# Fused attention and maxout FFN on one core: q and k transposed once on TensorE for groups 3 to 6, x of batch 1 on TensorE, output weights loaded later

## The chip, the cores and the metric

One core of one Trainium2 chip. The metric is the device time of one execution in microseconds (us), the median of several runs. Each run also reports a span (first to last instruction, about 1.9 us less than the device time) and the mean granted TensorE clock. A run over 1.5% above the fastest of its kernel is called slow and is left out of every ratio here.

Engines: PE is TensorE's matmuls, PEld its weight loads, DVE is VectorE, ACT is ScalarE, POOL is GpSimd, SP is SyncE, which here issues DMAs. A trailing q (POOLq, SPq) marks an engine's sequencer, for example when it issues a DMA. TensorE's results go to PSUM in this kernel, and another engine copies them out (an evacuation or eviction; in after the VectorE copies `hT<-p_i` are 48, of 0.62 us each). KT and QT are the transposed k and q, AV is the product of attention and v, and the up work or up pieces are the products with w1, w2 and w3.

## The reference, cut to what matters

```python
# q, k, v: (8 batches, 12 heads, 448 rows, 64)
scores = scale * q @ k.T
m = max(scores)
e = exp(scores - m)
attn = e / (sum(e) + exp(-m) + 1e-9)
x = (attn @ v) as (8 * 448, 768)
h = max(x @ w1, x @ w2, x @ w3)      # 768 x 768 each
out = h @ w_out                      # (3584, 768), float32
```

## The kernel before

The heads are taken in 24 groups of four heads, three groups to a batch; group `i` belongs to batch `i // 3`. Groups 0 to 2 are done in two halves, E and O, so that the FFN of batch 0 can start early; from group 3 on, each group takes three "visits" of score units. Between the steps of attention, `fill` puts pieces of FFN work (up projection, then output projection) into TensorE's program. The order in the program is the order in which an engine runs its instructions in the traces here, and a waiting instruction holds up those behind it.

The kernel's scores take q and k with the head dimension on partitions, in two arrangements of q. Groups 0 to 5 were transposed on TensorE, both arrangements of q (15 transposes) and k (7):

```python
PE_QK = 6          # groups below this are transposed on TensorE

def transpose_pe(i, pr, pool, k_eng, q_engs):     # pr 0 and 1: two halves
    ...
    kj = (0, 1, 2) if pr == 0 else (3, 4, 5, 6)
    qt = (-1, 1, 3, 5, 0, 2, 4, 6) if pr == 0 else (8, 10, 12, 7, 9, 11, 13)
    ...                                            # transposes to PSUM, then copies to KT, QT
```

From group 6 on, a DMA transpose makes one arrangement and GpSimd copies the shifted one (`shift_q`). x goes through DMA transposes from batch 1 on. The loads are issued in order by GpSimd:

```python
for n, (part, g) in enumerate(parts):     # E0 E1 E2 O0 O1 O2
    ...
    if n == 1:
        load_weight(2)
    if n == 2:
        load_v(3)
        load_qk(4)
        load_weight(3)                     # the output weights
    if n == 4:
        load_v(4)
        load_qk(5)
        transpose_pe(3, 0, ps_s, DV, (DV,))
...
for i in range(3, NI):
    ...
    for vi, units in enumerate(visits):
        scores(i, ej, units)
        ...
        if vi > 0 and i + 1 < PE_QK:       # the next group's q and k, in visits 1 and 2
            fill(per / 2)
            transpose_pe(i + 1, vi - 1, ps_s, DV, (DV,))
            fill(per / 2)
        else:
            fill(per)
```

The softmax here doesn't subtract the row's maximum and nothing guards it: scores larger than these inputs give would overflow.

Of the kernel before, what the change touches and what calls it, by code (L numbers as in the profile page):

```python
# [21 lines left out]
def kernel(  # L22
# [29 lines left out]
    scale = 1.0 / math.sqrt(D)  # L52


    PE_QK = 6
    NEB = 2
    NV = 3

# [9 lines left out]
    )  # L68

    cpool = ctx.enter_context(tc.tile_pool(name="const", bufs=1))  # L70
    ld_pool = ctx.enter_context(tc.tile_pool(name="ld", bufs=4))
    att_pool = ctx.enter_context(tc.tile_pool(name="att", bufs=3))
    small = ctx.enter_context(tc.tile_pool(name="small", bufs=3))
    xn_pool = ctx.enter_context(tc.tile_pool(name="xn", bufs=3))
# [12 lines left out]

    groups = [(b, g) for b in range(B) for g in range(NG)]
    raw = {}

    def load_qk(i, names="kq", prs=(0, NP)):
        b, g = groups[i]
        tiles = raw.setdefault(i, {})
        for nm in names:
            if nm not in tiles:
                t = ld_pool.tile([P, NP * T + 2, D], MMDT, tag="ld_" + nm, name="ld_" + nm)
                if nm == "q" and i < PE_QK:
                    nc.vector.memset(t[:, 0 : NP * T + 2 : NP * T + 1, :], 0.0)
                tiles[nm] = t
            src = {"q": q, "k": k}[nm][b].rearrange("h s d -> (h s) d")  # L100
            src = src.rearrange("(g r x t) d -> g x r (t d)", g=NG, r=NP, x=P)[g]
            p0, p1 = prs
            nc.gpsimd.dma_start(  # L103
                out=tiles[nm][:, 1 : NP * T + 1].rearrange("x (r t) d -> x r (t d)", r=NP)[:, p0:p1],
                in_=src[:, p0:p1],
            )

    def load_v(i):
        b, g = groups[i]
        t = ld_pool.tile([P, GH, 5, D], MMDT, tag="ld_v", name="ld_v")  # L110
        raw.setdefault(i, {})["v"] = t
        src = v[b].rearrange("(g h) (p t) d -> g p h (t d)", g=NG, t=T)[g]
        nc.gpsimd.dma_start(  # L113
            out=t[0:HP, :, 1:5].rearrange("p h t d -> p h (t d)"), in_=src[:, :, 0 : 4 * D]
        )
        nc.gpsimd.dma_start(  # L116
            out=t[HP:P, :, 0:4].rearrange("p h t d -> p h (t d)"), in_=src[:, :, 3 * D : T * D]
        )
# [53 lines left out]
    def transpose_pe(i, pr, pool, k_eng, q_engs):  # L172
# [30 lines left out]
        for e, eng in enumerate(q_engs):  # L203
            a, b = e * n * 128, min((e + 1) * n, len(qt)) * 128
            evac(eng, QT[i][:, q0 + a : q0 + b], tps[1][:, a:b])

    def transpose_dma(i):
        KT[i] = att_pool.tile([P, T * 128], MMDT, tag="KT", name="KT")
        QT[i] = att_pool.tile([P, (NB + 1) * 128], MMDT, tag="QT", name="QT")
        for dst, nm, o in ((QT[i], "q", 4), (KT[i], "k", 0)):  # L210
            nc.sync.dma_start_transpose(
                out=dst[:, o * 128 : (o + T) * 128].rearrange("p (j x) -> p j x", x=P),
                in_=raw[i].pop(nm)[:, 1 : NB + 1].rearrange("x t d -> x (t d)"),
            )

    def shift_q(i, eng):
# [135 lines left out]
        )  # L352

    def prep_v(i, eng):
        t = raw[i].pop("v")
        vx, vt = v_buf[i % NV], vt_buf[i % NV]
        eng.tensor_copy(out=vx[:, :, :, 0:D], in_=t[:, :, 1:4, :])  # L357
        t2 = t.rearrange("p (r h) t d -> p r h t d", r=NP)
        eng.tensor_copy(out=vt[0:HP, :, 0:D], in_=t2[0:HP, :, 0, 4, :])
        eng.tensor_copy(out=vt[HP:P, :, 0:D], in_=t2[HP:P, :, 1, 0, :])  # L360
# [6 lines left out]
    def x_transpose_pe(i, part):  # L367
        b, g = groups[i]
        ws = (0, 1) if part == "E" else (2, 3)
        qn, q0 = (NE, 0) if part == "E" else (NO, NE)  # L370
        tp = ps_b.tile([128, NP, 2, 128], MMDT, tag="b", name="xtp")
        for pr in range(NP):
            for j, w in enumerate(ws):
                nc.tensor.transpose(  # L374
                    out=tp[:, pr, j, :],
                    in_=xn[i][:, pr, w].rearrange("p h d -> p (h d)"),
                    identity=ident16,
                )
        dst = xt_tile(b)[:, 2 * g : 2 * g + 2, q0 : q0 + qn]
        nc.vector.tensor_copy(out=dst, in_=tp.rearrange("p a j s -> p a (j s)")[:, :, 0:qn])  # L380

    def x_transpose_dma(i):
        b, g = groups[i]
# [27 lines left out]
        else:  # L411
            nc.vector.tensor_tensor(out=dst, in0=dst, in1=src, op=ALU.max)  # L412

    NH = 2
    NW = DM // NH
    order = (0, 2, 4, 6, 1, 3, 5)

    def out_piece(bp, t, nh):
        if nh == 0:
            outs[0] = out_pool.tile([128, DM], FP32, tag="o_sb", name="o_sb")  # L420
        o_sb = outs[0]
        op_ps = ps_b.tile([128, 512], FP32, tag="b", name="op_ps")
        for fc in range(NFC):
            nc.tensor.matmul(  # L424
                out=op_ps[:, 0:NW],
                lhsT=hT[bp][:, fc, ts(t, 128)],
                rhs=wout_sb[:, fc, ts(nh, NW)],
                start=(fc == 0),
                stop=(fc == NFC - 1),
            )  # L430
        nc.vector.tensor_scalar(  # L431
            out=o_sb[:, ts(nh, NW)],
            in0=op_ps[:, 0:NW],
            scalar1=1.0 / LAMBDA,
            scalar2=None,
            op0=ALU.mult,
        )
        if nh == NH - 1:
            for half in range(2):
                n = 2 * t + half  # L440
                b = 2 * bp + n // T
                rows = out[b * S : (b + 1) * S].rearrange("(p t) m -> t p m", t=T)
                nc.sync.dma_start(out=rows[order[n % T]], in_=o_sb[half * HP : half * HP + HP])


    UP = NDC * (S + 6)
    OUT = NFC * (NW + 6)
    pieces = []

    def add_up(b, q0, qn, order):  # L450
# [3 lines left out]
            pieces.append((up_piece, (b, fcs, i, q0, qn), NDC * w * (qn + 6)))  # L454

    def add_out(b):
        for t in range(0, 3) if b % 2 == 0 else range(3, 7):
            for nh in range(NH):
                pieces.append((out_piece, (b // 2, t, nh), OUT))

    def add_batch(b):
        add_up(b, 0, S, [(i, fc) for fc in range(NFC) for i in range(3)])
# [27 lines left out]

    parts = [(part, g) for part in "EO" for g in range(NG)]
    PW = {"E": (0, 1), "O": (2, 3), "EO": (0, 1, 2, 3)}
    UPE = 9 * 2 * NDC * (NE + 6) / 12

    def av(i, ej, pr, part):
        av_tail(i, ej, pr, PW[part])
# [2 lines left out]
    for n, (part, g) in enumerate(parts):  # L499
        ej = n % NEB  # L500
        pp, pg = parts[n - 1] if n > 0 else (None, None)
        step = UPE if n > 2 else 0
        nxt = g + 1 if part == "E" and g < NG - 1 else None
        scores(g, ej, (0, 1), part)
        if n != 3:
# [5 lines left out]
        if n == 3:  # L511
            av(pg, 1 - ej, 1, pp)
            scores(g, ej, (2, 3), part)
        fill(step)
        if nxt is not None and n > 0:
            transpose_pe(nxt, 0, ps_b, AC, (DV,))
        fill(step)
        scores(g, ej, (4, 5), part)
        scores(g, ej, (6,), part)
        if n == 0:  # L520
            warm(4)
            transpose_pe(nxt, 0, ps_b, DV, (DV,))
        if n == 3:
            x_transpose_pe(pg, pp)
            add_up(0, 0, NE, [(i, f) for i in range(3) for f in (0, 2, 4)])
        if nxt is not None:
            transpose_pe(nxt, 1, ps_b, DV, (DV,))
        if n > 0 and n != 3:
            av(pg, 1 - ej, 1, pp)
        fill(step)  # L530
        if n == 5:
            transpose_pe(3, 1, ps_s, DV, (DV,))
        fill(step)
        if n == 0:
            prep_v(0, DV)
        if n == 1:
            load_weight(2)
        if n == 2:
            load_v(3)
            load_qk(4)  # L540
            load_weight(3)
        if n == 4:
            load_v(4)
            load_qk(5)
            transpose_pe(3, 0, ps_s, DV, (DV,))


    visits = ((0, 1), (2, 3), (4, 5, 6))
    adds = {3 * (3 * b + 4) + 1: b for b in range(1, B - 1)}

    def share(n):

        nxt = min([a for a in adds if a > n], default=3 * NI + 2)
        return left() / (nxt - n)

    for i in range(3, NI):
        ej, pj = (i + 1) % NEB, i % NEB
        first = i == 3
        if i + 2 < NI and i + 2 >= PE_QK:
            transpose_dma(i + 2)  # L560
        if first:
            load_v(5)
            load_qk(6)
        elif i + 2 < NI:
            load_v(i + 2)
            if i + 3 < NI:
                load_qk(i + 3)
        for vi, units in enumerate(visits):
            n = 3 * i + vi
            scores(i, ej, units)  # L570
            if vi < 2:
                av(i - 1, pj, vi, "O" if first else "EO")
            if vi == 1:
                prep_v(i, nc.vector if i < PE_QK else nc.gpsimd)
                if not first:
                    x_transpose_dma(i - 1)
            if n in adds:
                add_batch(adds[n])
            per = UPE if first and vi < 2 else share(n)
            if vi == 0 and first:  # L580
                x_transpose_pe(1, "O")
            if vi == 2 and first:
                fill(per / 2)
                x_transpose_pe(i - 1, "O")
                add_up(0, NE, NO, [(w, f) for w in range(3) for f in (0, 2, 4)])
                add_out(0)
                per = share(n)
            if vi > 0 and i + 1 < PE_QK:
                fill(per / 2)
                transpose_pe(i + 1, vi - 1, ps_s, DV, (DV,))  # L590
                fill(per / 2)
            else:
                fill(per)
        if i + 2 < NI and i + 2 >= PE_QK:
            shift_q(i + 2, nc.gpsimd)

    av(NI - 1, NI % NEB, 0, "EO")
    av(NI - 1, NI % NEB, 1, "EO")
# [34 lines left out]
```

## Time and profile before

The median was 343.53 us (three runs, 343.49 to 343.95). Lines of the profile page of the kernel before: the span, the busy time of each engine with its share of the span, and the chain of work that ended last, by engine.

```profile
span 343.9 us, 9746 instructions
PE 329.0 (96%) x4157; PEld 198.2 (58%) x4157; DVE 189.3 (55%) x418; ACT 146.4 (43%) x174; POOL 139.7 (41%) x247
...
PE 87%; DMA 5%; DVE 3%; ACT 2%; issue 1%; POOL 0%; SPq 0%; ACTq 0%; DVEq 0%; POOLq 0%
```

TensorE is busy for 96% of the span, and most of the chain is TensorE's own work. A gain has to come from TensorE's waits or from its instructions. The next view is the busy time of each engine by stretch of time. Its columns are the stretch, its length, then busy us and number of instructions of each engine, the granted TensorE clock, the DMA share and GB/s.

```profile
0.00:5.64 5.64, 3.75 (x10) 1.22 (x11) 0.70 (x12) 1.28 (x1) 4.50 (x12) 1.00 0.57 84
5.64:24.87 19.23, 16.19 (x316) 11.47 (x317) 11.34 (x36) 13.26 (x17) 15.10 (x26) 1.00 1.21 187
24.87:62.00 37.13, 34.19 (x582) 28.61 (x583) 23.74 (x62) 18.13 (x24) 16.31 (x26) 1.00 1.23 195
62.00:304.00 242.00, 240.15 (x3067) 138.24 (x3058) 133.38 (x276) 113.72 (x133) 103.76 (x186) 1.00 0.96 137
304.00:338.74 34.74, 34.74 (x195) 18.69 (x193) 19.60 (x33) 0.00 (x0) 0.00 (x0) 1.00 0.26 66
```

### The profile page before, as it was taken

The page shows a single profiled execution, that of the slowest core. Times are in us where ns is not written, and L with a number is a line of the kernel's source. Part 1 is how long each engine was busy: PE and PEld are TensorE (multiplying, and loading weights), DVE is VectorE, ACT ScalarE, POOL GpSimd, SP SyncE. Part 2 cuts the span into 40 slices and gives each one's busy share as a digit, 9 for nine tenths or more (in the row PEclk, how much of TensorE's full clock was granted, in tenths as well). Part 3 has the DMA queues.
Part 4 walks back from the last instruction along what each step waited for, and adds up shares of the span by engine and source line. Part 5 has one row for each costly group of instructions (what it writes and reads, how often), then busy time and mean ns, then how long its engine had stood idle before and what let it go on. Part 6 is the DMA issues. An engine that isn't in the chain of part 4 may idle for free.

```text
span 343.9 us, 9746 instructions
## 1 busy us (share of the span) xinstructions
PE 329.0 (96%) x4157; PEld 198.2 (58%) x4157; DVE 189.3 (55%) x418; ACT 146.4 (43%) x174; POOL 139.7 (41%) x247
## 2 busy tenths in 40 slices
PE   7889988999999989999999999999999999999994
PEld 3568767855555645556555555556555655465552
DVE  2565666755456456556556556556556555565552
ACT  2773366574544444444444444444444443300000
POOL 8583452906749055373374245472455000000000
PEclk9999999999999999999999999999999999999998
DMA  7999999999999999979966999989980460123006
GB/s 103 186 207 210 205 201 163 171 118 207 206 186 118 127 239 124 154 107 218 161 86 97 162 212 139 155 98 219 148 138 15 124 124 3 31 67 103 2 17 167
DMA packets 89499, 47.42 MB, mean 138 GB/s; under 512 B 58224, under 2 KB 85872, under 8 KB 89456
## 3 DMA queue, kind: packets, MB, share of 16 engines
q0 software_dynamic: 29392, 22.03, 48.0%
q1 hardware_dynamic: 60064, 24.78, 43.3%
q8 instruction: 32, 0.52, 0.6%
q14 instruction: 11, 0.09, 0.1%
HBM read 44.04 MB, written 11.01 MB: 160 GB/s over the span
## 4 chain that ended last, share of the span: by engine, by line
PE 87%; DMA 5%; DVE 3%; ACT 2%; issue 1%; POOL 0%; SPq 0%; ACTq 0%; DVEq 0%; POOLq 0%
PE p_i L401 48%; PE op_ps L424 14%; PE stp L274 11%; PE avp L331 11%; DMA out_dram<-o_sb 2%; PE avp L314 2%; ACT e L294 2%; PE trT L181 2%; DMA xT<-xn 1%; DMA ld_k<-in_k_dram 1%; DVE QT L170 1%; DVE o_sb L431 0%; DVE xn L347 0%; DVE xT L380 0%; PE xtp L374 0%
## 5 line engine op out<-in xcount | busy, mean ns | idle before, releaser
L294 ACT ACTIVATE e<-stp 128x896 f16<-128x896 f32 (+4 forms) x171 | 144.0, 902 | 146.7 <-PE stp L274 146.7
L401 PE MATMUL p_i<-xT,w 128*128 128x448 f16 (+2 forms) x972 | 173.7, 332 | 2.0 <-DVE o_sb L431 1.4
L401 PEld LDWEIGHTS <-w 128*128 128x128 f16 x972 | 89.9, 98 | 70.0 <-issue 7.5
L412 DVE TENSOR_TENSOR hT<-hT,p_i 128x448 f16<-128x448 f16 (+2 forms) x96 | 59.6, 621 | 43.4 <-PE p_i L401 43.2
L219 POOL COPY QT<-QT 64x384 f16<-64x384 f16 (+1 forms) x72 | 40.2, 558 | 103.0 <-DMA QT<-ld_q 63.8
L424 PE MATMUL op_ps<-w,hT 128*128 128x384 f16 x336 | 58.3, 326 | 0.0
L274 PE MATMUL stp<-QT,KT 64*64 64x448 f16 (+2 forms) x756 | 47.9, 338 | 3.4 <-ACT e L294 1.9
L431 DVE TENSOR_SCALAR o_sb<-op_ps 128x384 f32<-128x384 f32 x56 | 30.9, 556 | 28.4 <-PE op_ps L424 22.9
L331 PE MATMUL avp<-vx,e 128*128 128x65 f16 x1152 | 45.4, 193 | 0.0
L424 PEld LDWEIGHTS <-hT 128*128 128x128 f16 x336 | 31.7, 98 | 23.1 <-issue 2.1
L410 DVE CAST hT<-p_i 128x448 f16<-128x448 f32 (+2 forms) x48 | 30.0, 624 | 24.3 <-PE p_i L401 24.2
L331 PEld LDWEIGHTS <-e 128*128 128x128 f16 x1152 | 38.8, 97 | 2.2
L347 DVE TENSOR_TENSOR xn<-avp,rb 128x512 f16<-128x512 f32 (+1 forms) x54 | 34.1, 632 | 1.9
L274 PEld LDWEIGHTS <-KT 64*64 64x64 f16 x756 | 15.8, 105 | 28.2 <-issue 23.8
L341 DVE TENSOR_SCALAR rb<-avp 128x8 f32<-128x8 f32 (+1 forms) x54 | 8.9, 165 | 39.1 <-PE avp L331 39.1
L314 PEld LDWEIGHTS <-e 64*64 64x64 f16 x768 | 14.5, 107 | 9.3 <-DVE QT L170 0.8
L103 POOL DMA_DIRECT2D ld_q<-in_q_dram x24 | 17.7, 736 | 4.2 <-PE trT L181 1.9
L103 POOL DMA_DIRECT2D ld_k<-in_k_dram x25 | 17.9, 716 | 3.1 <-PE p_i L401 1.5
L357 POOL COPY vx<-ld_v 128x768 f16<-128x768 f16 x20 | 16.4, 821 | 5.1 <-issue 2.6
L314 PE MATMUL avp<-vt,e 64*64 64x65 f16 x768 | 15.7, 193 | 1.5 <-DVE QT L170 0.6
L113 POOL DMA_DIRECT2D ld_v<-in_v_dram x24 | 15.2, 633 | 3.2 <-DVE xT L380 1.7
L116 POOL DMA_DIRECT2D ld_v<-in_v_dram x24 | 15.2, 634 | 2.1 <-DMA w<-in_moe_w_out_dram 1.2
(33 smaller groups left out, 83.9 us busy)
## 6 DMA issues: line engine op xcount, KB each, us to landing
out_dram<-o_sb SPq DMA_DIRECT2D x56, 192.0 KB, 3.4
ld_v<-in_v_dram POOLq DMA_DIRECT2D x48, 128.0 KB, 4.8
ld_q<-in_q_dram POOLq DMA_DIRECT2D x24, 224.0 KB, 7.5
ld_k<-in_k_dram POOLq DMA_DIRECT2D x23, 224.0 KB, 6.8
w<-in_moe_w_dram POOLq DMA_DIRECT2D x9, 384.0 KB, 9.8
w<-in_moe_w_out_dram POOLq DMA_DIRECT2D x3, 384.0 KB, 10.9
xT<-xn SPq DMA_TRANSPOSE x21, 4.4
QT<-ld_q SPq DMA_TRANSPOSE x18, 6.6
```

Source lines behind the costliest of these rows:

```text
L103: nc.gpsimd.dma_start(out=tiles[nm][:, 1 : NP * T + 1].rearrange("x (r t) d -> x r (t d)", r=NP)[:, p0:p1], in_=src[:, p0:p1],)
L219: eng.tensor_copy(out=t[d0 : d0 + HP, o * 128 : (o + n) * 128], in_=t[s0 : s0 + HP, a * 128 : (a + n) * 128],)
L274: nc.tensor.matmul(out=stp[half * HP : half * HP + HP, par, j * qn : (j + 1) * qn], lhsT=k_block(i, pr, h2, x[half]), rhs=q_cols(i, pr, h2 ...
L294: nc.scalar.activation(out=dst, in_=src, func=AF.Exp, scale=scale)
L314: nc.tensor.matmul(out=ps[half * HP : half * HP + HP, hh, j * D1 : (j + 1) * D1], lhsT=eF[hh * HP : hh * HP + HP, o : o + HP], rhs=vt[hh * ...
L331: nc.tensor.matmul(out=ps[:, hh, j * D1 : (j + 1) * D1], lhsT=eF[:, o : o + 128], rhs=vx[:, 2 * pr + hh, (x[0]), 0:D1], start=False, stop= ...
L347: nc.vector.tensor_tensor(out=xn[i][:, pr, ws[0] : ws[0] + nw].rearrange("p j h d -> p h j d"), in0=acc[:, :, :, 0:D], in1=rb[:, :, 0:nw]. ...
L401: nc.tensor.matmul(out=p_i[:, j * qn : (j + 1) * qn], lhsT=w_sb[i][:, dc, ts(fc, 128)], rhs=xT[b][:, dc, q0 : q0 + qn], start=(dc == 0), s ...
L410: nc.vector.tensor_copy(out=dst, in_=src)
L412: nc.vector.tensor_tensor(out=dst, in0=dst, in1=src, op=ALU.max)
L424: nc.tensor.matmul(out=op_ps[:, 0:NW], lhsT=hT[bp][:, fc, ts(t, 128)], rhs=wout_sb[:, fc, ts(nh, NW)], start=(fc == 0), stop=(fc == NFC - 1),)
L431: nc.vector.tensor_scalar(out=o_sb[:, ts(nh, NW)], in0=op_ps[:, 0:NW], scalar1=1.0 / LAMBDA, scalar2=None, op0=ALU.mult,)
```

## The change: intent and diff

The intent was to relieve TensorE and VectorE early on. Groups 3 to 6 get one arrangement of q from TensorE (7 transposes for q, 7 for k; groups 3 to 5 had 22 there, group 6 none), and GpSimd makes the other. The transposes move from the three-buffer PSUM pool that scores use to the two-buffer pool of the FFN. x of batch 1 moves from DMA to TensorE. The output weights load after group 5, not before. The last output tile goes out in three pieces over two queues. The fill is spread with an allowance for AV work. The core of the diff (cuts marked with `...`):

```diff
-    PE_QK = 6
+    PE_QK = 7
+    NF = 3
+    PE_X = 2
 ...
+    def transpose_once(i, nm, eng):
 ...                                   # 7 transposes of q or of k into one ps_b tile, one copy by eng
+    def x_transpose_all(i):
 ...                                   # x of one group: 8 transposes on TensorE
+            if b == B - 1 and t == 6:
+                cuts = [(0, NW, (sy, sy)), (NW, 256, (sc, sc)), (NW + 256, 128, (sy, sc))]
 ...
         if n == 2:
             load_v(3)
             load_qk(4)
-            load_weight(3)
         if n == 4:
+            shift_q(3, nc.gpsimd)
             load_v(4)
             load_qk(5)
-            transpose_pe(3, 0, ps_s, DV, (DV,))
+            load_weight(3)
 ...
-            if vi > 0 and i + 1 < PE_QK:
-                fill(per / 2)
-                transpose_pe(i + 1, vi - 1, ps_s, DV, (DV,))
-                fill(per / 2)
-            else:
+            if first and vi == 1:
+                transpose_once(i + 1, "q", AC)
                 fill(per)
-        if i + 2 < NI and i + 2 >= PE_QK:
+                transpose_once(i + 1, "k", DV)
+                per = 0
+            elif i + 1 < PE_QK and vi < 2:
+                transpose_once(i + 1, "qk"[vi], (AC, DV)[vi])
+            fill(per)
+        if i + 1 < PE_QK:
+            shift_q(i + 1, nc.gpsimd)
 ...
+    AVC = 2200                         # allowance for AV work in share()
```

Here `first` is `i == 3`.

More of the change, by code (lines that the diff above doesn't have):

```diff
@@ L70 @@
     cpool = ctx.enter_context(tc.tile_pool(name="const", bufs=1))
-    ld_pool = ctx.enter_context(tc.tile_pool(name="ld", bufs=4))
     att_pool = ctx.enter_context(tc.tile_pool(name="att", bufs=3))
@@ L89 @@
     raw = {}
+    NL = 4
+    ld_bufs = {
+        nm: [
+            cpool.tile([P, GH, 5, D] if nm == "v" else [P, NP * T + 2, D], MMDT, name=f"ld_{nm}{j}")
+            for j in range(NL)
+        ]
+        for nm in "kqv"
+    }
     def load_qk(i, names="kq", prs=(0, NP)):
@@ L95, in load_qk @@
             if nm not in tiles:
-                t = ld_pool.tile([P, NP * T + 2, D], MMDT, tag="ld_" + nm, name="ld_" + nm)
-                if nm == "q" and i < PE_QK:
+                t = ld_bufs[nm][i % NL]
+                if nm == "q" and i < NF:
                     nc.vector.memset(t[:, 0 : NP * T + 2 : NP * T + 1, :], 0.0)
@@ L109, in load_v @@
         b, g = groups[i]
-        t = ld_pool.tile([P, GH, 5, D], MMDT, tag="ld_v", name="ld_v")
+        t = ld_bufs["v"][i % NL]
         raw.setdefault(i, {})["v"] = t
@@ L205, in transpose_pe @@
             evac(eng, QT[i][:, q0 + a : q0 + b], tps[1][:, a:b])
+    def transpose_once(i, nm, eng):
+        if i not in KT:
+            KT[i] = att_pool.tile([P, T * 128], MMDT, tag="KT", name="KT")
+            QT[i] = att_pool.tile([P, (NB + 1) * 128], MMDT, tag="QT", name="QT")
+        tp = ps_b.tile([128, 1024], MMDT, tag="b", name="trT")
+        for b in range(T):
+            nc.tensor.transpose(
+                out=tp[:, ts(b, 128)],
+                in_=raw[i][nm][:, 2 * b + 1 : 2 * b + 3, :].rearrange("x t d -> x (t d)"),
+                identity=ident16,
+            )
+        dst = KT[i][:, 0 : T * 128] if nm == "k" else QT[i][:, 4 * 128 : (4 + T) * 128]
+        evac(eng, dst, tp[:, 0 : T * 128])
     def transpose_dma(i):
@@ L212, in transpose_dma @@
                 out=dst[:, o * 128 : (o + T) * 128].rearrange("p (j x) -> p j x", x=P),
-                in_=raw[i].pop(nm)[:, 1 : NB + 1].rearrange("x t d -> x (t d)"),
+                in_=raw[i][nm][:, 1 : NB + 1].rearrange("x t d -> x (t d)"),
             )
@@ L354, in prep_v @@
     def prep_v(i, eng):
-        t = raw[i].pop("v")
+        t = raw[i]["v"]
         vx, vt = v_buf[i % NV], vt_buf[i % NV]
@@ L380, in x_transpose_pe @@
         nc.vector.tensor_copy(out=dst, in_=tp.rearrange("p a j s -> p a (j s)")[:, :, 0:qn])
+    def x_transpose_all(i):
+        b, g = groups[i]
+        tp = ps_b.tile([128, NP, 4, 128], MMDT, tag="b", name="xtp")
+        for pr in range(NP):
+            for w in range(4):
+                nc.tensor.transpose(
+                    out=tp[:, pr, w, :],
+                    in_=xn[i][:, pr, w].rearrange("p h d -> p (h d)"),
+                    identity=ident16,
+                )
+        dst = xt_tile(b)[:, 2 * g : 2 * g + 2, 0:S]
+        nc.vector.tensor_copy(out=dst, in_=tp.rearrange("p a j s -> p a (j s)")[:, :, 0:S])
     def x_transpose_dma(i):
@@ L412, in up_piece, with out_piece @@
             nc.vector.tensor_tensor(out=dst, in0=dst, in1=src, op=ALU.max)
-    NH = 2
-    NW = DM // NH
+    NW = DM // 2
     order = (0, 2, 4, 6, 1, 3, 5)
-    def out_piece(bp, t, nh):
-        if nh == 0:
+    def out_piece(bp, t, c, w, queues):
+        if c == 0:
             outs[0] = out_pool.tile([128, DM], FP32, tag="o_sb", name="o_sb")
+            outs[1] = 0
         o_sb = outs[0]
@@ L424, in out_piece @@
             nc.tensor.matmul(
-                out=op_ps[:, 0:NW],
+                out=op_ps[:, 0:w],
                 lhsT=hT[bp][:, fc, ts(t, 128)],
-                rhs=wout_sb[:, fc, ts(nh, NW)],
+                rhs=wout_sb[:, fc, c : c + w],
                 start=(fc == 0),
@@ L431, in out_piece @@
         nc.vector.tensor_scalar(
-            out=o_sb[:, ts(nh, NW)],
-            in0=op_ps[:, 0:NW],
-            scalar1=1.0 / LAMBDA,
-            scalar2=None,
+            out=o_sb[:, c : c + w], in0=op_ps[:, 0:w], scalar1=1.0 / LAMBDA, scalar2=None,
             op0=ALU.mult,
         )
-        if nh == NH - 1:
-            for half in range(2):
-                n = 2 * t + half
-                b = 2 * bp + n // T
-                rows = out[b * S : (b + 1) * S].rearrange("(p t) m -> t p m", t=T)
-                nc.sync.dma_start(out=rows[order[n % T]], in_=o_sb[half * HP : half * HP + HP])
+        if queues is None:
+            return
+        for half in range(2):
+            n = 2 * t + half
+            b = 2 * bp + n // T
+            rows = out[b * S : (b + 1) * S].rearrange("(p t) m -> t p m", t=T)[order[n % T]]
+            queues[half].dma_start(
+                out=rows[:, outs[1] : c + w], in_=o_sb[half * HP : half * HP + HP, outs[1] : c + w]
+            )
+        outs[1] = c + w
     UP = NDC * (S + 6)
-    OUT = NFC * (NW + 6)
     pieces = []
@@ L456, in add_out @@
     def add_out(b):
+        sy, sc = nc.sync, nc.scalar
         for t in range(0, 3) if b % 2 == 0 else range(3, 7):
-            for nh in range(NH):
-                pieces.append((out_piece, (b // 2, t, nh), OUT))
+            cuts = [(0, NW, None), (NW, NW, (sy, sy))]
+            if b == B - 1 and t == 6:
+                cuts = [(0, NW, (sy, sy)), (NW, 256, (sc, sc)), (NW + 256, 128, (sy, sc))]
+            for c, w, queues in cuts:
+                pieces.append((out_piece, (b // 2, t, c, w, queues), NFC * (w + 6)))
     def add_batch(b):
@@ L492 @@
     PW = {"E": (0, 1), "O": (2, 3), "EO": (0, 1, 2, 3)}
-    UPE = 9 * 2 * NDC * (NE + 6) / 12
+    UPE = 2 * NDC * (NE + 6)
     def av(i, ej, pr, part):
@@ L501 @@
         pp, pg = parts[n - 1] if n > 0 else (None, None)
-        step = UPE if n > 2 else 0
+        step = UPE if n > 3 else 0
         nxt = g + 1 if part == "E" and g < NG - 1 else None
@@ L513 @@
             scores(g, ej, (2, 3), part)
+        if n == 4:
+            transpose_once(3, "q", AC)
         fill(step)
@@ L516 @@
             transpose_pe(nxt, 0, ps_b, AC, (DV,))
-        fill(step)
         scores(g, ej, (4, 5), part)
@@ L522 @@
             transpose_pe(nxt, 0, ps_b, DV, (DV,))
+            prep_v(0, DV)
         if n == 3:
@@ L525 @@
             add_up(0, 0, NE, [(i, f) for i in range(3) for f in (0, 2, 4)])
+            fill(UPE)
         if nxt is not None:
-            transpose_pe(nxt, 1, ps_b, DV, (DV,))
+            transpose_pe(nxt, 1, ps_b, DV, (AC, DV) if n == 0 else (DV,))
         if n > 0 and n != 3:
             av(pg, 1 - ej, 1, pp)
+        if n == 4:
+            transpose_once(3, "k", AC)
         fill(step)
-        if n == 5:
-            transpose_pe(3, 1, ps_s, DV, (DV,))
-        fill(step)
-        if n == 0:
-            prep_v(0, DV)
         if n == 1:
@@ L540, with load_more @@
             load_qk(4)
-            load_weight(3)
         if n == 4:
+            shift_q(3, nc.gpsimd)
             load_v(4)
             load_qk(5)
-            transpose_pe(3, 0, ps_s, DV, (DV,))
+            load_weight(3)
     visits = ((0, 1), (2, 3), (4, 5, 6))
-    adds = {3 * (3 * b + 4) + 1: b for b in range(1, B - 1)}
+    adds = {3 * (3 * b + 4) + (b >= PE_X): b for b in range(1, B - 1)}
+    AVC = 2200
     def share(n):
         nxt = min([a for a in adds if a > n], default=3 * NI + 2)
-        return left() / (nxt - n)
+        rest = range(n, nxt)
+        sums = [AVC if m % 3 < 2 and m < 3 * NI else 0 for m in rest]
+        return max(0, (left() + sum(sums)) / len(rest) - sums[0])
+    def load_more(iv, iq):
+        if iv < NI:
+            load_v(iv)
+        if iq < NI:
+            load_qk(iq)
     for i in range(3, NI):
@@ L558 @@
         first = i == 3
-        if i + 2 < NI and i + 2 >= PE_QK:
+        if PE_QK <= i + 2 < NI:
             transpose_dma(i + 2)
         if first:
-            load_v(5)
-            load_qk(6)
-        elif i + 2 < NI:
             load_v(i + 2)
-            if i + 3 < NI:
-                load_qk(i + 3)
         for vi, units in enumerate(visits):
@@ L570 @@
             scores(i, ej, units)
+            if i == 4 and vi == 0:
+                prep_v(i, DV)
             if vi < 2:
                 av(i - 1, pj, vi, "O" if first else "EO")
-            if vi == 1:
-                prep_v(i, nc.vector if i < PE_QK else nc.gpsimd)
-                if not first:
-                    x_transpose_dma(i - 1)
+            if vi == 1 and i > 3 * PE_X:
+                x_transpose_dma(i - 1)
             if n in adds:
@@ L582 @@
             if vi == 2 and first:
+                x_transpose_pe(i - 1, "O")
                 fill(per / 2)
-                x_transpose_pe(i - 1, "O")
+                prep_v(i, DV)
                 add_up(0, NE, NO, [(w, f) for w in range(3) for f in (0, 2, 4)])
@@ L587 @@
                 per = share(n)
-            if vi > 0 and i + 1 < PE_QK:
-                fill(per / 2)
-                transpose_pe(i + 1, vi - 1, ps_s, DV, (DV,))
-                fill(per / 2)
-            else:
-                fill(per)
-        if i + 2 < NI and i + 2 >= PE_QK:
+            if vi == 2 and 3 < i <= 3 * PE_X:
+                x_transpose_all(i - 1)
+            if first and vi == 1:
+                transpose_once(i + 1, "q", AC)
+                fill(per)
+                transpose_once(i + 1, "k", DV)
[5 more added lines that the diff above has]
+            shift_q(i + 1, nc.gpsimd)
+        if first:
+            load_qk(i + 3)
+        if i < 5:
+            load_more(i + 3, i + 4)
+        if 5 <= i + 1 < NI:
+            prep_v(i + 1, nc.gpsimd)
+        if PE_QK <= i + 2 < NI:
             shift_q(i + 2, nc.gpsimd)
+        if i >= 5:
+            load_more(i + 3, i + 4)
     av(NI - 1, NI % NEB, 0, "EO")
```

## The prediction

> **What bounds the kernel now.** TensorE. The page gives PE busy 329.0 of 343.9 us (96%); the chain that ended last lies 87% on PE; the granted clock is 1.0 until the last 5 us. The table of stretches puts the PE idle time at 1.9 us before 5.6 us, 3.0 from 5.6 to 24.9, 2.9 from 24.9 to 62, 1.9 from 62 to 304, none to 338.7, and 5.2 after the last matmul. From 62 us on TensorE is at its issue pitch (448-column matmuls start 189 ns apart), so only two waits can be won there: 0.41 us at 82 us for the DMA transpose of x, and 1.44 us at 122 us, where an output buffer waited 3.6 us for its write, behind DMA transposes in the SP queue.
>
> **What the change does.**
> - Groups 3 to 5: 22 TensorE transposes each become 14; GpSimd makes the shifted half (2.39 us a group in the timeline). Group 6: none becomes 14. x of batch 1: 24 more. Net +14. They start 55 ns apart: +0.8 us on TensorE as a whole, but -1.3 us before 62 us.
> - DVE evacuation for groups 3 to 5: 2.1 us a group becomes 0.6; ScalarE takes a 128x896 copy, estimated at 0.9 us from its 128x512 copy (0.60).
> - These transposes leave the PSUM pool that scores and AV use. In the timeline TensorE waits for a ScalarE exp near such a transpose: 0.34, 0.89, 0.89 us (45.5, 47.2, 57.8 us). Most of this should go, and the 0.59 us at 34.9 us where AV waited for QT's evacuation.
> - Five DMA transposes less (q and k of group 6, three of x); they landed after a median of 4.4 to 6.6 us. The wait at 82 us should go.
> - Output weights load behind group 5: issued near 45 us, landing in 11 us, first used at 68 us, so no new wait.
> - The tail: the last tile is cut in 384+256+128 columns over two queues. Now: eviction 0.56 us, two issues of 0.58 us in one queue, landing 3.4 us (median).[...] I estimate 1.2 us saved.
>
> **Sum.** 5.6 to 25 us: -0.4 (split evacuation of q, earlier V). 25 to 62: -2.2 of waits, -1.3 of transposes. 62 to 304: +2.1 (38 x 55 ns), -1.3 of waits. Tail: -1.2. About -4, of which some comes back as small waits for ScalarE's later evacuations out of the two-buffer pool.
>
> **Prediction: 339.8 us, 337.2 to 342.2 (8 in 10).** Faster by over 2%: 0.06; within 2%: 0.92; slower: 0.02.
>
> **What would show it right.** 122 transposes to QT/KT and 48 of x on PE, DMA transposes 17, 17 and 18; PE idle between 25 and 62 us below 1.5 us; PE waits for exps (three, 1.9 us) under 0.7; after the last matmul about 4 us instead of 5.2; the stretch from 62 to 304 within 1 us of before.
>
> **What would make it wrong.** ScalarE's copies stand behind exps, so both buffers of the small pool stay full and up pieces wait; GpSimd's shift blocks its own queue, so loads of groups 5 to 7 come late; TensorE waits for KT/QT of group 7 at about 75 us. The wait at 122 us may remain, as nothing there is changed directly: then 341.

The sum: its terms come to -4.3 us (-0.4 - 2.2 - 1.3 + 2.1 - 1.3 - 1.2), given as about -4.

## More of the kernel before

From 24.87 to 62 us TensorE lacks 2.94 us of work (37.13 - 34.19). That stretch holds the end of batch 0 and groups 3 and 4, and there the change was expected to gain most. From 62 us on little is missing. These are lines of the timeline there (start us, length us, what, and in brackets the idle time before it and what ended it): GpSimd issues the load of q of group 4, and TensorE first uses it.

```profile
29.97 0.70 POOL L103 DMA_DIRECT2D ld_q<-in_q_dram  x1 [1.24 <-DVE xn L347]
...
45.85 0.33 PE L181 MATMUL trT<-ident,ld_k 128*128 128x128 f16 x3 [0.34 <-ACT e L294]
...
46.01 0.61 PE L181 MATMUL trT<-ident,ld_q 128*128 128x128 f16 x8
```

The trace has this load landing at 40.6 us and its first use at 46.0, so before the change there were over 5 us of slack.

## The result, and the profile after

The kernel after took 345.87 us (345.52 to 346.23, four runs) against 343.74 us (343.49 to 344.11, four runs) before. The ratio is 1.0061, 95% interval 1.0044 to 1.0079. Ratios here are the mean time of one kernel's fast runs over that of the other's of the same rounds, so they are not quite the ratios of the medians. The change costs 0.6% where 1.1% was expected as a gain.

Two of the lines shown of the page before, in the page after:

```profile
PE 331.3 (96%) x4184; PEld 200.3 (58%) x4184; DVE 187.1 (54%) x407; ACT 151.7 (44%) x181; POOL 147.3 (43%) x262
...
PE 88%; DMA 4%; ACT 4%; issue 1%; DVE 1%; POOL 0%; ACTq 0%; POOLq 0%
```

They say little. The stretches say where:

```profile
24.87:62.00 37.13, 33.99 (x592) 27.92 (x591) 20.05 (x51) 22.67 (x30) 22.59 (x37) 0.95 1.17 183
62.00:304.00 242.00, 241.90 (x3071) 140.01 (x3068) 135.25 (x276) 113.70 (x134) 104.66 (x188) 1.00 0.92 133
```

From 62 to 304 us TensorE has almost no idle time left (0.10 us). From 24.87 to 62 us it still lacks 3.14 us, and the granted clock, 1.00 before, has a mean of 0.95. The view of TensorE's waits of the kernel after has one entry above all others (total us, times, longest):

```profile
PE trT L224 <- DMA ld_q<-in_q_dram: 2.7, 1, 2.7
PE warm L165 <- DVE wz L141: 1.2, 1, 1.2
PE stp L299 <- DVE xn L372: 0.7, 1, 0.7
...
PE stp L299 <- ACT e L319: 0.2, 1, 0.2
```

The chain that ended last, in order of time, in the same place (start us, us, what):

```profile
28.88 0.40 PE stp L299 x12
29.28 0.07 issue
29.35 10.84 DMA ld_q<-in_q_dram
40.19 0.05 issue
40.23 0.93 PE trT L224 x7
41.16 2.23 PE p_i L439 x12
```

And the timeline of the kernel after, TensorE and the load:

```profile
29.35 0.70 POOL L113 DMA_DIRECT2D ld_q<-in_q_dram  x1 [1.22 <-PE stp L299]
...
40.23 0.93 PE L224 MATMUL trT<-ident,ld_q 128*128 128x128 f16 x7 [2.71 <-DMA ld_q<-in_q_dram]
...
40.95 2.44 PE L439 MATMUL p_i<-xT,w 128*128 128x256 f16 x12
...
44.28 0.55 PE L224 MATMUL trT<-ident,ld_q 128*128 128x128 f16 x7
```

Three things are to be read here.

- The load was issued (29.35) and landed (40.2) as before (29.97 and 40.6). TensorE asked for it at 37.5 us instead of 46.0.
- The seven transposes of `ld_q` are there **twice**, at 40.23 and at 44.28. In the code, visit 0 of group 3 does not match `first and vi == 1`, falls into the `elif`, and transposes q of group 4; visit 1 does it again. The first set is a leftover: its result is overwritten by the same values. I call them the stray transposes. They stand ahead of `fill(per)`, so the twelve up matmuls which could have covered the wait stood behind them.
- The same twelve up matmuls and seven transposes take far longer than elsewhere: 0.93 us against 0.55 for the transposes, 2.44 against 1.47 (the 1.47 is the twelve-matmul up piece in other rows). In three stretches of 3.41 us, cut at the two changes of the granted clock at 39.50 and 42.91 us, the clock (third column from the right) reads 1.00, 0.50, 1.00:

```profile
36.09:39.50 3.41, 1.43 (x34) 0.98 (x32) 1.72 (x5) 1.73 (x2) 2.46 (x4) 1.00 1.34 199
39.50:42.91 3.41, 2.68 (x17) 2.12 (x18) 0.00 (x0) 0.92 (x1) 1.59 (x3) 0.50 1.27 205
42.91:46.32 3.41, 3.23 (x51) 2.53 (x50) 1.60 (x5) 2.50 (x3) 0.00 (x0) 1.00 1.16 211
```

So the clock was half for 3.41 us. It fell 1.98 us after TensorE went idle (37.52 us), and TensorE was busy for 1.43 us of the 3.41 us ahead of the fall. After the last matmul it took longer: 3.29 us in before (338.74 to 342.03) and 4.56 us in after (338.73 to 343.29). More on this stands with best and best_qk5.

### The profile page after: what moved, and what is told of

Read it like the earlier page. It is cut to its first block, busy times and chain, and to the rows that moved or that the text cites. A ratio compares the mean times of both kernels' runs of the same rounds, so it can differ in the third digit from the quotient of the medians.

```text
span 343.9 us, 9827 instructions
## 1 busy us (share of the span) xinstructions
PE 331.3 (96%) x4184; PEld 200.3 (58%) x4184; DVE 187.1 (54%) x407; ACT 151.7 (44%) x181; POOL 147.3 (43%) x262
## 4 chain that ended last, share of the span: by engine, by line
PE 88%; DMA 4%; ACT 4%; issue 1%; DVE 1%; POOL 0%; ACTq 0%; POOLq 0%
PE p_i L439 46%; PE op_ps L463 16%; PE stp L299 11%; PE avp L356 10%; DMA ld_q<-in_q_dram 3%; ACT e L319 3%; PE avp L339 2%; ACT QT L178 1%; DMA ld_k<-in_k_dram 1%; PE trT L191 1%; PE trT L224 1%; PE xtp L412 0%; DVE QT L180 0%; PE warm L165 0%; DVE xn L372 0%
## 5 line engine op out<-in xcount | busy, mean ns | idle before, releaser
L244 POOL COPY QT<-QT 64x384 f16<-64x384 f16 (+1 forms) x84 | 46.7, 556 | 101.2 <-DMA QT<-ld_q 72.2
L463 PE MATMUL op_ps<-w,hT 128*128 128x384 f16 (+2 forms) x342 | 58.3, 324 | 0.0
L470 DVE TENSOR_SCALAR o_sb<-op_ps 128x384 f32<-128x384 f32 (+2 forms) x57 | 31.1, 549 | 26.1 <-PE op_ps L463 22.0
L382 POOL COPY vx<-ld_v 128x768 f16<-128x768 f16 x21 | 17.2, 820 | 6.6 <-issue 4.1
```

Source lines behind the costliest of these rows:

```text
L244: eng.tensor_copy(out=t[d0 : d0 + HP, o * 128 : (o + n) * 128], in_=t[s0 : s0 + HP, a * 128 : (a + n) * 128],)
L463: nc.tensor.matmul(out=op_ps[:, 0:w], lhsT=hT[bp][:, fc, ts(t, 128)], rhs=wout_sb[:, fc, c : c + w], start=(fc == 0), stop=(fc == NFC - 1),)
L470: nc.vector.tensor_scalar(out=o_sb[:, c : c + w], in0=op_ps[:, 0:w], scalar1=1.0 / LAMBDA, scalar2=None, op0=ALU.mult,)
```

## The experiments

Theory 1: the stray transposes wait for a load that is not due yet, and the idle time then halves the clock (0.50 in the stretch above); the rest of the change gains about what was predicted. Rivals: the load is too late for the new schedule whatever the strays do; the low clock is unrelated or costs nothing; transposes in the two-buffer pool cost by themselves; moving the weights or the x work costs.

Sixteen kernels ran, all correct. `us` is the median of all runs, the ratio is to the kernel before in the same rounds.

| label | us | ratio (95% interval) |
|---|---|---|
| after | 345.87 | 1.0061 (1.0044 to 1.0079) |
| no_stray | 341.13 | 0.9921 (0.9906 to 0.9936) |
| fill_gap | 344.38 | 1.0009 (0.9992 to 1.0027) |
| early_q4 | 342.09 | 0.9949 (0.9934 to 0.9964) |
| ns_full_tr | 344.24 | 1.0006 (0.9984 to 1.0028) |
| ns_old_tail | 341.30 | 0.9914 (0.9896 to 0.9933) |
| ns_x_dma | 340.00 | 0.9881 (0.9854 to 0.9908), one slow run of six |
| ns_qk6 | 339.97 | 0.9881 (0.9861 to 0.9900) |
| ns_avc0 | 341.73 | 0.9934 (0.9915 to 0.9953) |
| ns_wout_early | 342.70 | 0.9968 (0.9949 to 0.9986) |
| best | 343.42 | 0.9979 (0.9948 to 1.0010), one slow run of six |
| best_qk5 | 343.73 | 1.0005 (0.9969 to 1.0042) |
| best_x_pe | 339.40 | 0.9861 (0.9843 to 0.9880) |
| best_g6_pe | 340.35 | 0.9896 (0.9870 to 0.9922) |
| best_late_q4 | 342.58 | 0.9860 (0.9832 to 0.9889), three slow runs of six |
| tail_split | 340.29 | 0.9894 (0.9872 to 0.9916) |

### The kernel before once more (before_again)

No edit.

> The kernel before, unchanged, for a second profile. Its only profile so far belonged to an execution of 345.79 us, while its other runs took 343.5 to 344.1. Expected: if the 1.44 us wait at 122 us and the 0.41 us wait at 82 us are not in every execution, this one shows fewer of them and a span near 341.7 us; if the profile itself costs 2 us, the waits are as before and the span is again 343.9.

It took 344.36 us with a span of 342.4 us. The wait at 122 us is not in its list of waits, nor the 0.41 us at 82 us. The timed runs of before in all rounds had spans of mostly 341.5 to 342.5 us. So the profile that the prediction read belonged to a longer execution of this kernel than usual (though not a slow one by the rule above): 1.44 us of its idle time is not in the second profile, and was counted as something to win.

### The stray transposes removed (no_stray)

```diff
-            elif i + 1 < PE_QK and vi < 2:
+            elif not first and i + 1 < PE_QK and vi < 2:
```

> After, without the transposes of q of group 4 that stand in the first visit of group 3 (the same seven are made again in the second visit; the first set is a leftover). Theory 1: these seven are the first work that needs q of group 4, 2.7 us before it lands, and after the idle time the granted clock is half for 3.4 us: without them the wait and the low clock go, 4 to 4.5 us less than after, 341.3 to 342. Rival (the load of q of group 4 is simply too late for the new schedule): the wait only moves to the next transposes of that q, and 0 to 1.5 us are won.

341.13 us, 4.7 us less than after, a little more than theory 1 expected. The rival does not hold. It is not wholly wrong: some of the wait moved to the transposes that are needed, as the waits of this kernel show.

```profile
PE trT L224 <- DMA ld_q<-in_q_dram: 0.7, 1, 0.7
```

The up piece that stood behind the strays now runs ahead of the load's landing: in the timeline of this kernel it starts at 37.13 us; the kernel after was idle from 37.5 us on.

```profile
37.13 1.47 PE L439 MATMUL p_i<-xT,w 128*128 128x256 f16 x12
...
40.38 0.56 PE L224 MATMUL trT<-ident,ld_q 128*128 128x128 f16 x7 [0.73 <-DMA ld_q<-in_q_dram]
```

The stretch of the kernel after with 3.14 us of idle time and a mean clock of 0.95 has 1.07 us of idle time and a clock of 1.00 here:

```profile
24.87:62.00 37.13, 36.06 (x663) 30.30 (x663) 21.69 (x55) 24.19 (x32) 25.10 (x42) 1.00 1.24 200
```

So one line of the change turns a gain of 0.8% into a loss of 0.6%.

### The idle time filled, the strays kept (fill_gap)

```diff
             elif i + 1 < PE_QK and vi < 2:
+                warm(12 if first else 0)      # 12 matmuls of 512 columns on zeros
                 transpose_once(i + 1, "qk"[vi], (AC, DV)[vi])
```

> After, with 12 matmuls on zeros just ahead of the early transposes, which fill the 2.7 us in which TensorE sat idle. If the clock drop comes from the idle time and costs time of its own: clock stays 1.0 throughout, 1.5 to 1.9 us less than after. If the clock drop is not linked to the idle time, or costs nothing: the drop is still there, or the time stays within 0.4 us of after.

The clock reads 1.00 from 36.47 to 43.29 us, across the strays and the up piece, in the profile, which is of the slowest of the four runs (345.47 us; the load landed at 41.2 us there), and the median is 1.5 us below after (the ratios, 1.0061 and 1.0009, say 0.0052 x 344 = 1.8 us). TensorE arrives at the up piece no earlier than in after (41.68 us against 40.95), so this is what the low clock costs. The trace of after says the same from the other side: from 40.23 us to the next scores at 43.32 the strays and the up piece take 3.09 us, against 0.40 + 1.31 = 1.71 us in no_stray (starts 40.38, 40.78 and, for the next set, 42.09), so 1.4 us.

### The load earlier, the strays kept (early_q4)

```diff
         if n == 1:
+            load_qk(4)
             load_weight(2)
         if n == 2:
             load_v(3)
-            load_qk(4)
```

> After, with the loads of k and q of group 4 issued before those of the third up weight rather than after; the early transposes stay. Theory 1 (late data, not the transposes themselves): wait gone and clock 1.0, 3.8 to 4.3 us less than after, so 0.2 to 0.5 us more than without the early transposes. Rival (the transposes cost by themselves, or block the small PSUM pool): less than 1 us won.

342.09 us: 3.8 us below after, as expected, and no low clock before the last of the page's 40 slices. But it is 1.0 us above no_stray where I had expected it below. The strays are not free even with the data there: seven transposes are 0.4 us (7 x 55 ns), and the waits of this kernel show two more, one of the up piece for a copy of x, and one for a ScalarE copy ahead of the transposes of k that follow the second set (after has this one too).

```profile
PE p_i L439 <- DVE xT L405: 0.6, 1, 0.6
...
PE trT L224 <- ACT QT L178: 0.3, 1, 0.3
```

So the 4.8 us that the strays cost (ratios 1.0061 and 0.9921) are about 2.7 us of wait, 1.4 to 1.8 us of low clock, and the rest the transposes and their waits, less the 0.7 us of wait that no_stray still has.

### All 22 transposes again (ns_full_tr)

On no_stray:

```diff
-            transpose_once(3, "q", AC)        # and likewise "k", and for i + 1
+            transpose_pe(3, 0, ps_s, DV, (DV,))
...
-        if i + 1 < PE_QK:
-            shift_q(i + 1, nc.gpsimd)
```

(`NF` is 4 here, so that the padding is zeroed in all four buffers.)

> The kernel without the stray transposes, but with all 22 transposes on TensorE for groups 3 to 6, evacuated by VectorE through the three-buffer PSUM pool as before, and nothing on GpSimd. If transposing once pays by TensorE's own time: 32 transposes more at 55 ns, 1.8 us, and the waits for exps near them come back (up to 1.5 us): 342.9 to 344.5, against 341.13 without the edit. If the gain came from elsewhere: under 342.

344.24 us: the whole gain of no_stray is gone, 2.9 us by the ratios. Transposing once, with what belongs to it, is what the change earns; this edit also gives back the PSUM pool, the engines of the copies and GpSimd's shift, so these were not told apart. Of the 2.9 us, 32 transposes at 55 ns are an estimated 1.8 us (seven take 0.55 us from first start to last end, and the last alone 0.22, so they start 55 ns apart). The other 1.1 us may be in the waits: the profile has 0.8 us for exps, which no_stray's does not, and 0.8 us for copies of QT instead of 0.3, but not no_stray's 0.7 us for q of group 4.

```profile
PE trT L191 <- ACT e L319: 0.8, 3, 0.3
PE stp L299 <- DVE QT L180: 0.8, 2, 0.5
```

### The tail as before (ns_old_tail), and split otherwise (tail_split)

On no_stray, the last tile as in before (the special case removed), and:

```diff
-                cuts = [(0, NW, (sy, sy)), (NW, 256, (sc, sc)), (NW + 256, 128, (sy, sc))]
+                cuts = [(0, NW, (sy, sc)), (NW, NW, (sy, sc))]
```

> The kernel without the stray transposes, with the last output tile as before (two pieces of 384 columns, two transfers in the SP queue). In the traces the new tail's last transfer is issued only at 340.0 us, behind four others, and lands at 342.80 against 342.53 before, at the same end of the matmuls within 0.1 us. So I expect the old tail to be as fast or faster: 340.8 to 341.2. If the prediction's 1.2 us for the tail were right, 342.3.

> The kernel without the stray transposes (341.13), where the last tile is in two pieces of 384 columns and each piece is sent half from the SP queue, half from the ScalarE queue. The last transfer is then issued 0.5 us earlier than with both in one queue, with nothing ahead of it: the last landing 3.2 us after the last matmul rather than 3.6 to 4.2; 340.4 to 340.8. If the write's own time decides, not the issue: 341.1.

The tail of before is as fast (0.9914 against 0.9921, well inside the intervals). In the trace of after the last landing comes 4.07 us after the last matmul ends, in before 3.79. A queue issues one transfer after another, each 0.47 to 0.60 us (the last ten of after), and the six transfers of the three pieces stood three deep in each queue: the last one was issued at 340.02 us, 0.96 us after its eviction was done. With two pieces, each half to one queue, nothing stands ahead: the last eviction ends at 334.46 us, and the last issues end 0.5 and 0.6 us later (334.99 and 335.07; in after 1.2 and 1.5 us later, 340.27 and 340.57 after 339.06). The time is 0.9 us below no_stray by the ratios, whose intervals just overlap. So a gain of the split is likely, and its size is not shown.

### x of batch 1 and group 6 back to DMA, one at a time (ns_x_dma, ns_qk6)

On no_stray, `PE_X = 1`, and in the other `PE_QK = 6`.

> The kernel without the stray transposes, with x of batch 1 by DMA transpose again. TensorE saves 24 transposes at 55 ns, 1.3 us. If DMA transposes there cost TensorE no wait: 339.8 to 340.2. If they make it wait (as the 0.41 us at 82 us in one profile of before), or if the up work of batch 1 is held back: 341 or more.

> The kernel without the stray transposes, with q and k of group 6 by DMA transpose again. TensorE saves 14 transposes at 55 ns, 0.8 us: 340.4 if nothing waits for it. If the DMA transpose of group 6 is late, because it needs group 6's load by about 47 us: TensorE waits ahead of the scores of group 6[...]: 342 or more.

Each is 1.4 us faster by the ratios, near what TensorE saves in transposes (estimated at 1.3 and 0.8 us, 24 and 14 at 55 ns). The 0.7 us wait for q of group 4 is also absent from both profiles; it is absent from those of ns_old_tail and ns_avc0 too, whose code is the same there, so it rather belongs to one execution. No wait for x or for group 6 is there. So these two parts of the change cost time where the kernel runs well. ns_x_dma scatters, though: its fast runs go from 339.07 to 341.21 us, and its interval just touches that of no_stray.

### Output weights and the spread of the fill (ns_wout_early, ns_avc0)

On no_stray: the output weights ahead of group 5 as in before; and `AVC = 0`.

> The kernel without the stray transposes, with the output weights loaded ahead of group 5 as before. If their place matters: q and k of group 5 land some 8 us later, TensorE waits ahead of the transposes of group 5 near 48 us[...]: 342 to 345. If there is slack: within 0.4 us of 341.13. The wait for q of group 4 (0.7 us) is not touched by it.

> The kernel without the stray transposes, with the allowance for AV work in the share of filled work set to 0. The trace shows TensorE busy without a gap from 62 us on in both kernels, so how the fill is spread should not matter: 340.8 to 341.5. If the smoothing does pay: 342 or more.

The place of the weights matters: 1.6 us by the ratios. The transposes of q of group 5 start at 50.18 us, after a wait, instead of at 47.67 without one in no_stray.

```profile
PE trT L224 <- DMA ld_q<-in_q_dram: 1.6, 1, 1.6
```

A clause is cut from the expectation of ns_wout_early too: it took a low clock to follow from such a wait. None came: the mean granted clock of its profiled run is 0.998, where 3.41 us at half clock would leave 0.995 (an estimate: 1.7 of 342.2 us). Of the spread of the fill nothing can be said: 0.9934 against 0.9921, with intervals that overlap.

### The parts together (best, best_qk5)

best is no_stray with `PE_X = 1`, `PE_QK = 6`, the early load of group 4 and the tail of tail_split. best_qk5 has `PE_QK = 5` as well.

> The parts that the runs so far support, together: no stray transposes, x of batch 1 and group 6 by DMA transpose as before, loads of group 4 ahead of those of the third up weight, and the last output tile in two pieces, each sent half from the SP queue and half from the ScalarE queue. From 341.13: x -1.2, group 6 -0.8, no wait for q of group 4 -0.5 to -0.7, tail -0.5 to -0.7: 337.9 to 338.3 if the parts add. If they hide one another (the wait is gone in some of them already), 338.5 to 339.

> The same, with group 5 by DMA transpose as well: TensorE saves 14 transposes at 55 ns, 0.8 us, so 337.2 to 337.6 if the DMA transpose comes in time (its load is issued near 37 us, its scores start near 56 us). If it is late, or crowds the loads: slower than the run above.

Neither came near the time expected if the parts add. They do not add. The waits of best:

```profile
PE p_i L439 <- DMA xT<-xn: 3.0, 1, 3.0
PE warm L165 <- DVE wz L141: 1.2, 1, 1.2
PE stp L299 <- DMA KT<-ld_k: 1.2, 1, 1.2
```

With both on DMA, TensorE waits 3.0 us for x and 1.2 us for k of group 6. In best_qk5 it waits for k of group 5:

```profile
PE stp L299 <- DMA KT<-ld_k: 5.1, 1, 5.1
```

These two also show more of the clock. Stretches of 3.41 us, of best_qk5 (where the clock changes at 58.96 and 65.78 us), then of best, across its wait of 3.0 us:

```profile
55.54:58.96 3.42, 0.00 (x0) 0.00 (x0) 0.25 (x1) 0.00 (x0) 3.32 (x6) 1.00 1.38 193
58.96:62.37 3.41, 2.08 (x42) 1.63 (x43) 0.00 (x0) 1.38 (x2) 3.04 (x7) 0.50 1.31 189
62.37:65.78 3.41, 3.41 (x46) 2.64 (x43) 1.61 (x4) 0.66 (x2) 2.79 (x6) 0.50 1.65 180
65.78:69.20 3.42, 3.42 (x70) 2.78 (x63) 1.52 (x4) 2.40 (x4) 0.00 (x0) 1.00 1.08 196
```

```profile
76.83:80.24 3.41, 1.65 (x34) 1.12 (x29) 1.12 (x4) 1.56 (x2) 3.36 (x6) 1.00 1.31 160
80.24:83.65 3.41, 2.17 (x20) 0.94 (x19) 1.08 (x2) 0.07 (x1) 1.02 (x3) 1.00 1.16 297
```

In best the wait was longer than in after (3.00 us against 2.71) and the clock did not fall (1.00 in both stretches, 0.998 over the run). So the length of the wait alone does not decide. Of the two stretches of best 1.76 and 1.24 us were idle; of the stretch ahead of the half clock 1.98 us were in after, and all 3.42 in best_qk5. Whether that is what decides, these runs do not show. Nor is the length of the half clock fixed: in best_qk5 the first stretch at half clock was busy for 2.08 us and a second followed, 6.82 us in all; in after one that was busy for 2.68 us was the only one.

### Which part is at fault (best_x_pe, best_g6_pe, best_late_q4)

Each is best with one part taken back: `PE_X = 2`; `PE_QK = 7`; the load of group 4 as in after.

> The combined kernel of 343.4 us, with x of batch 1 on TensorE again. It waited 3.0 us for xT by DMA and 1.2 us for KT of group 6 by DMA. If three more DMA transposes of x in one queue with those of groups 6 to 8 are at fault: both waits go, 339.0 to 339.8 us. If the earlier load alone is at fault: a wait for KT stays, 341 or more.

> The combined kernel, with group 6 on TensorE again, x of batch 1 by DMA. If only both together crowd the queue: 338.9 to 339.6. If x by DMA waits by itself: the wait for xT stays, with a large scatter between executions (one of six runs of x by DMA alone took 345.0).

> The combined kernel, with the loads of group 4 behind those of the third up weight, as in after. If the earlier load shifts the later loads into the DMA transposes: 338.2 to 338.8. If x and group 6 by DMA together are at fault: still 341 to 344, with waits for xT and KT.

With x of batch 1 on TensorE both DMA waits are gone, and all four runs lie between 338.98 and 339.67 us. This is the fastest kernel that is also steady: 1.4% below before, 2.0% below after (0.9861 / 1.0061). With group 6 on TensorE instead, runs go from 339.40 to 342.02 us; the profile has a wait of 1.2 us for an output buffer and none for x, so the wait for x expected there did not show. With the later load, three runs are fast (338.64 to 340.56; the profile, of the last of these, has a wait of 1.3 us for k of group 6 and none for x) and three are slow; slow runs explain nothing here. So x of batch 1 by DMA is the part common to all kernels here with a wide scatter: alone it mostly paid, and together with group 6 by DMA and the early load it gave the gain back. With the late load it did not in the three fast runs, so the early load has a share in it that these runs do not separate. What delays that one transpose by DMA (in best it was issued at 72.1 us and the up work that needs it started at 81.5; the DMA transposes of x there took 2.7 to 11.3 us to land, 5.2 at the median) was not settled by these runs.

## Why the prediction was wrong, point by point

- **What bounds the kernel**: right. TensorE is busy for 96% before and after.
- **"Groups 3 to 5: 22 TensorE transposes each become 14", 122 in all: this step failed.** The trace of after has 129 transposes of q and k (45 + 21 + 35 + 28, the counts after the x in the lines below; the numbers behind them are busy us, mean ns of one, and idle us before with what ended it), because group 4's q is made twice. The prediction took the count from the description, and did not walk the two branches through visit 0 of group 3. Removing the seven brings 122 and 341.13 us, inside the predicted range.

```profile
L191 PE MATMUL trT<-ident,ld_q 128*128 128x128 f16 x45 | 3.5, 219 | 0.4 <-DVE QT L180 0.4
L224 PE MATMUL trT<-ident,ld_q 128*128 128x128 f16 x35 | 3.1, 237 | 2.7 <-DMA ld_q<-in_q_dram 2.7
L224 PE MATMUL trT<-ident,ld_k 128*128 128x128 f16 x28 | 2.2, 218 | 0.3 <-ACT QT L178 0.3
L191 PE MATMUL trT<-ident,ld_k 128*128 128x128 f16 x21 | 2.2, 219 | 0.2
```

- **"25 to 62: -2.2 of waits"** went with it: TensorE's idle time there was 2.94 us before and 3.14 us after, as the wait of 2.71 us for q of group 4 took the place of those that went; without the strays it is 1.07 us.
- **"Output weights load behind group 5 ... no new wait", "loads of groups 5 to 7 come late"**: the prediction asked when the moved loads would land, but not when the moved consumers would ask. q of group 4 landed at 40.6 us before; any first use ahead of that waits. The list of what could go wrong named groups 5 to 7 and the small PSUM pool, but not group 4. The place of the weights turned out to be worth 1.6 us in the new schedule, which the prediction gave nothing.
- **The low clock** was not in the prediction at all. It cost 1.4 to 1.8 us on top of 2.7 us of wait.
- **Waits for exps under 0.7 us**: right, 0.2 us. **ScalarE's copy at 0.9 us**: right, 0.93. **PE idle from 25 to 62 us under 1.5 us**: 3.14 us in after, 1.07 us in no_stray (37.13 - 36.06). **x on TensorE: 48 transposes**, right.
- **"62 to 304: +2.1 (38 x 55 ns), -1.3 of waits"**: whether the transposes were sized right stays open: x and group 6 on TensorE cost 1.4 us each as measured one at a time, 2.8 together, of which up to 0.7 us each may be the wait for q of group 4 that these two profiles did not have. The wait of 1.44 us at 122 us was mostly not there to be won: the second profile of the same kernel does not have it.
- **"Tail: -1.2"**: mis-sized; it was 0. The last seven transfers of after land 2.2 to 2.8 us after they are issued, and no run here splits that into a fixed part and the rest. What the prediction missed is that cutting a tile makes more transfers, and that each holds its queue for about 0.55 us (0.52 to 0.60 for the last six).
- **The sum**: without the strays -2.7 us against a predicted -4; the tail and the wait at 122 us, 2.5 us together, were credited and never came. Transposing once brought 2.9 us, against 3.5 us that the prediction gave to the stretch from 25 to 62 us.

## What to carry to other kernels

When a change moves a consumer to an earlier place in an in-order program, look up in the trace when its data lands now; moving only the consumer turned over 5 us of slack into a wait of 2.71 us here, and independent work belongs ahead of it, not behind. Count the instructions that the changed control flow really makes, branch by branch (a count by line in the profile shows a doubled block at once). And price a wait of TensorE with the half clock that may follow it: after 2.71 us of wait in the kernel after it was half for 3.41 us and cost 1.4 to 1.8 us, after 3.00 us in best it did not come. Parts that each pay alone have to be run together before they are believed.
